# A recurrent-attention and Fourier-mix kernel: all engine streams in one list-scheduled order, with shared PSUM banks, a transposed state and sequential batches

## The chip, the cores and the metric

The kernel runs on one core of a Trainium2 chip. The metric is the device time of one execution in microseconds (us). A profile is one execution; its span is some 2 us shorter than the device time of the same run. Every timed comparison is made on one chip, beside runs of the kernel before.

The engines in the profile: PE is TensorE (matmuls), PEld its weight loads, DVE is VectorE, ACT is ScalarE, POOL is GpSimd, SP is the engine that issues most DMAs. Each works off its own stream of instructions in order.

## The reference, cut to what matters

For 4 batches, 8 heads, 768 time steps and head size 40, a recurrence with a 40x40 state per head:

```python
y[:, :, t] = einsum('bhd,bhde->bhe', rt, state)
Sa = einsum('bhde,bhe->bhd', state, at)
state = state * wt[:, :, None, :] - einsum('bhd,bhe->bhde', Sa, bt) + einsum('bhd,bhe->bhde', vt, kt)
```

Then, per batch, on x of 768x320 (the heads side by side): the real part of a two-dimensional Fourier transform is added to x, the rows are normalised, and an MLP (320 to 1280, relu, back to 320) is added.

## The kernel before

Both kernels split the 768 steps into 6 chunks of 128, so there are 24 chunks in all. For each chunk, **preparation** (no state needed) takes the logarithm of w, its running sum by a matmul with ones, the exponentials, scales k, b and a on GpSimd, transposes them on TensorE and forms three masked 128x128 products for each head. The **chain** (needs the state) solves for the chunk's corrections in two rounds, updates the state and gives y. When a batch is done, its **post** stage does Fourier transform, normalisation and MLP.

The parts that the argument touches:

```python
psP = ctx.enter_context(tc.tile_pool(name="psP", bufs=4, space=PSUM))
psA = ctx.enter_context(tc.tile_pool(name="psA", bufs=2, space=PSUM))
psM = ctx.enter_context(tc.tile_pool(name="psM", bufs=2, space=PSUM))
# ... preparation: decay row through DRAM, broadcast to 64 partitions, twice
nc.scalar.activation(flat(wl)[96:128], cum[96:128], Act.Exp)
nc.sync.dma_start(wd, wl[127:128].rearrange("p h d -> p (h d)"))
for e in range(2):
    nc.sync.dma_start(wm[i % 3][e * 64:(e + 1) * 64, :, e, :],
                      bass.AP(wd.tensor, wd.offset + e * D, [[0, 64], [2 * D, NP], [1, D]]))
# ... chain: new state, its bf16 copy, and the transposed copy that the next chunk's X needs
nc.vector.tensor_add(P, P, st[0])
nc.vector.tensor_tensor(s32, P, g["wm"], Alu.mult)
nc.scalar.copy(sc[:, :, :, :D], s32)
nc.tensor.transpose(...)                      # x4
nc.vector.tensor_copy(sT, pt)
# ... chain, last line: y of the chunk
nc.vector.tensor_tensor(xb[:, c, :], Y.rearrange("t h d -> t (h d)"), g["wp"], Alu.mult)
# ... the driver: batches 0 and 1 (then 2 and 3) interleaved, the second three chunks behind
order = []
for j in range(3 * (B + 1)):
    for sm in (0, 1):
        q = j - 3 * sm
        if 0 <= q < NCH * (B // 2):
            order.append((2 * (q // NCH) + sm, q % NCH))
for i, (bb, c) in enumerate(order):
    states[bb] = chain(bb, c, i, gs.pop(i), states[bb], xbs[bb], not pend)
    # ... load chunk i + 3, prepare chunk i + 2, two pieces of a pending post stage
```

The framework that builds the kernel reorders each engine's stream with a scheduler of its own; the written order guides it.

## Time and profile before

| | before |
|---|---|
| time, median (all runs) | 421.11 us (420.61 to 422.29) |
| span of the profile | 419.9 us |
| PE / DVE / ACT / POOL busy | 77% / 51% / 51% / 46% |
| mean granted TensorE clock | 0.877 |

First the engine table of the kernel before (busy us, share of the span, instructions), then two of the rows of the view in 40 slices (busy tenths of PE, and granted TensorE clock in tenths), one line of the DMA queues (packets, MB, share of 16 engines) and the shares of the chain of waits that ended last:

```profile
PE 325.0 (77%) x3636; PEld 223.0 (53%) x3636; DVE 215.2 (51%) x430; ACT 213.6 (51%) x448; POOL 191.8 (46%) x279
...
PE   1657778854887877788798787688798976998796
...
PEclk9996988895888896599899999659959998799999
...
q1 hardware_dynamic: 170728, 37.07, 45.5%
...
PE 35%; POOL 13%; DVE 12%; issue 10%; ACT 10%; DMA 3%; SPq 1%; POOLq 0%; ACTq 0%; DVEq 0%
```

No engine is full, and the chain that decides the time passes through all of them. The clock row shows stretches of 5 and 6, where TensorE was granted half its clock for most of a slice.

The last instruction of each chunk, the multiply by wp, marks progress. It starts first at 38.7 and last at 359.4 us. Cut there, the kernel has three stages.

The middle stage holds 23 chunk-to-chunk steps in 320.7 us, 13.9 us each, and TensorE is busy for 79% of it. The last stage is 60.5 us, when all recurrences are over.

What a step waits for is seen in the chain of waits in order of time (start us, length us, engine, what), here around 300 us of the kernel before:

```profile
300.32 1.08 ACT M_4890 L251 x2
...
301.54 0.26 POOL M_4890 L180
...
302.59 0.86 POOL t__91 L125
303.45 0.18 POOL t__91 L126
...
304.24 0.86 POOL t__91 L127
...
305.14 1.46 PE pt L143 x12
...
308.07 0.68 DVE A_4989 L161
```

It goes from the copies of M (chunk's chain) on ScalarE to its mask on GpSimd, then to GpSimd's three products for a *later* chunk, which stand behind that mask in GpSimd's stream, to that chunk's transposes, and to VectorE's masks. Preparation that needs no state waits behind chain work.

### The profile page before, as it was taken

How to read it: one execution, taken by the hardware profiler on the slowest of the kernel's cores; microseconds unless marked ns; L12 is line 12 of the kernel's file. 1: busy time of each engine (PE TensorE's matmuls, PEld its weight loads, DVE VectorE, ACT ScalarE, POOL GpSimd, SP SyncE). 2: the span in 40 equal slices, each digit the busy share in tenths (PEclk: the TensorE clock that was granted, in tenths of full speed). 3: DMA queues.
4: the chain of work that ended last, by engine and by line, in shares of the span. 5: the costliest groups of instructions: out<-in, count | busy, mean ns of one | idle time of the engine just before them, and what ended most of it. 6: DMA issues, size and time to landing. Idle time of an engine off the chain costs nothing.

```text
span 419.9 us, 9289 instructions
## 1 busy us (share of the span) xinstructions
PE 325.0 (77%) x3636; PEld 223.0 (53%) x3636; DVE 215.2 (51%) x430; ACT 213.6 (51%) x448; POOL 191.8 (46%) x279
## 2 busy tenths in 40 slices
PE   1657778854887877788798787688798976998796
PEld 0435455542666655645555565464574654556353
DVE  4342555796646477725515658854352568112611
ACT  2334546565545654574483675457455454742352
POOL 4886834671647652631523786443333355202100
PEclk9996988895888896599899999659959998799999
DMA  9999685852555755616506576323140300222011
GB/s 153 183 147 161 111 143 96 142 92 43 97 101 148 167 98 87 101 27 126 95 18 133 133 177 119 55 49 53 53 148 19 86 2 2 94 94 95 0 48 47
DMA packets 172435, 39.29 MB, mean 94 GB/s; under 512 B 161556, under 2 KB 172072, under 8 KB 172392
## 3 DMA queue, kind: packets, MB, share of 16 engines
q1 hardware_dynamic: 170728, 37.07, 45.5%
q0 software_dynamic: 1664, 1.64, 2.4%
q8 instruction: 28, 0.46, 0.4%
q14 instruction: 15, 0.12, 0.1%
HBM read 32.44 MB, written 7.89 MB: 96 GB/s over the span
## 4 chain that ended last, share of the span: by engine, by line
PE 35%; POOL 13%; DVE 12%; issue 10%; ACT 10%; DMA 3%; SPq 1%; POOLq 0%; ACTq 0%; DVEq 0%
PE ph L184 7%; PE po L184 7%; PE pt L143 4%; ACT hm L363 2%; PE X L184 2%; PE pt L355 1%; POOL t__103 L127 1%; POOL rs L343 1%; POOL t__103 L126 1%; ACT snT L248 1%; POOL t__97 L125 1%; DMA xd<-xb 1%; PE pt L238 1%; PE pt L246 1%; DMA x__4928<-in_w_dram 1%
## 5 line engine op out<-in xcount | busy, mean ns | idle before, releaser
L184 PE MATMUL ph<-unT,w1sb 128*128 128x384 bf16 x240 | 50.1, 340 | 3.7 <-ACT unT L356 1.3
L363 ACT ACTIVATE hm<-ph 128x384 bf16<-128x384 f32 x80 | 39.1, 494 | 19.5 <-PE ph L184 18.6
L155 ACT COPY vT<-pt 128x512 bf16<-128x512 bf16 x24 | 14.1, 587 | 53.4 <-PE pt L143 51.3
L184 PE MATMUL po<-w2sb,hm 128*128 128x320 bf16 x240 | 35.6, 299 | 0.2 <-ACT hm L363 0.2
L184 PEld LDWEIGHTS <-w1sb 128*128 128x128 bf16 x240 | 22.9, 102 | 22.3 <-issue 11.3
L122 DVE TENSOR_TENSOR wp<-cum,logw 128x320 f32<-128x320 f32 x24 | 11.7, 487 | 43.6 <-ACT rw L120 43.6
L374 DVE TENSOR_TENSOR ot<-po,u 128x320 f32<-128x320 f32 x24 | 11.8, 490 | 40.0 <-PE po L184 40.0
L143 PE MATMUL pt<-ident_78,t__91 128*128 128x128 bf16 x160 | 17.1, 263 | 17.0 <-POOL t__91 L125 7.9
L149 DVE COPY kbT<-pt 128x1024 bf16<-128x1024 bf16 x24 | 16.5, 689 | 22.3 <-PE pt L143 22.2
L184 PEld LDWEIGHTS <-hm 128*128 128x128 bf16 x240 | 22.5, 98 | 10.2 <-issue 0.7
L118 PE MATMUL cum<-logw,ut_ones 128*128 128x320 f32 x48 | 24.6, 601 | 4.3 <-ACT logw L116 4.3
L209 DVE TENSOR_TENSOR dx<-X,xs 128x320 bf16<-128x320 f32 x24 | 11.7, 488 | 28.0 <-PE X L184 24.5
L143 PEld LDWEIGHTS <-t__91 128*128 128x128 bf16 x160 | 11.9, 117 | 21.9 <-POOL t__91 L125 9.7
L143 PE MATMUL pt<-ident_78,t__103 128*128 128x128 bf16 x160 | 15.8, 250 | 9.9 <-POOL t__103 L127 3.6
L152 DVE COPY arT<-pt 128x1024 bf16<-128x1024 bf16 x24 | 16.6, 692 | 12.6 <-PE pt L143 12.6
L174 PEld LDWEIGHTS <-vT 64*128 64x128 bf16 x192 | 13.8, 100 | 15.2 <-issue 13.5
L143 PE MATMUL pt<-ident_78,t__97 128*128 128x128 bf16 x160 | 14.7, 244 | 6.5 <-POOL t__97 L127 2.5
L248 ACT COPY snT<-pt 128x512 bf16<-128x512 bf16 x24 | 14.1, 587 | 9.7 <-PE pt L246 9.1
L345 DVE TENSOR_SCALAR un<-u,mv,rs 128x320 bf16<-128x320 f32 x24 | 14.7, 654 | 8.0 <-POOL rs L343 8.0
L310 POOL COPY zzr<-zz 128x256 bf16<-128x256 bf16 x16 | 6.0, 399 | 27.9 <-ACT zz L307 27.9
L143 PEld LDWEIGHTS <-t__103 128*128 128x128 bf16 x160 | 11.2, 112 | 13.4 <-POOL t__103 L127 5.0
L174 PEld LDWEIGHTS <-kbT 64*128 64x128 bf16 x384 | 13.7, 108 | 8.2 <-DVE arT L152 4.1
(1032 smaller groups left out, 928.4 us busy)
## 6 DMA issues: line engine op xcount, KB each, us to landing
xd<-xb SPq DMA_DIRECT2D x4, 960.0 KB
u<-xd SPq DMA_DIRECT2D x24, 160.0 KB, 2.9
out_dram<-ot SPq DMA_DIRECT2D x24, 160.0 KB, 1.9
w2sb<-in_moe_w_ch_dram POOLq DMA_DIRECT2D x1, 800.0 KB, 10.7
w1sb<-in_moe_w_ch_dram POOLq DMA_DIRECT2D x2, 320.0 KB, 6.1
t__95<-wd SPq DMA_DIRECT2D x16, 40.0 KB, 4.1
t__101<-wd SPq DMA_DIRECT2D x12, 40.0 KB, 3.1
t__107<-wd SPq DMA_DIRECT2D x12, 40.0 KB, 4.2
```

What stands on the lines that cost most here:

```text
L118: nc.tensor.matmul(cum, ut_ones, logw)
L122: nc.vector.tensor_sub(wp, cum, logw)
L143: nc.tensor.transpose(pt[:, j, q, :], s_[:, 2 * q:2 * q + 2, :].rearrange("t h d -> t (h d)"), ident16)
L149: nc.vector.tensor_copy(kbT, pt)
L152: nc.vector.tensor_copy(arT, pt)
L155: nc.scalar.copy(vT, pt[:, 0])
L174: nc.tensor.matmul(ps[e][:, q, :], lT[e * 64:(e + 1) * 64, q, :], rT[e * 64:(e + 1) * 64, q, :], start=(q == 0), stop=True, skip_group_che ...
L184: nc.tensor.matmul(o, l_, r_, start=first, stop=True, skip_group_check=True)
L248: nc.scalar.copy(snT, pt)
L345: nc.vector.tensor_scalar(un[:, ti], u[:, ti], mv[:, ti, 0:1], rs[:, ti:ti + 1], Alu.subtract, Alu.mult)
L363: nc.scalar.activation(hm, ph, Act.Relu)
L374: nc.vector.tensor_tensor(ot, po, u[:, ti], Alu.add)
```

## The change

Intent: plan all five streams together. The kernel records each operation with its engine, an estimated occupancy, the buffers it reads and writes, and a rank. A list scheduler in the kernel then picks, again and again, the operation that can start first (within a window of 0.12 us the better rank wins), binds buffers, and emits. The framework's scheduler is switched off. With it come: eight PSUM banks in one pool (at most 4 for preparation, at most 3 for post), batches one after another, a state kept transposed, the decay summed on TensorE, and warm-up matmuls on zeros where the plan sees TensorE idle. The core of the diff, with cuts marked:

```diff
+            for e in self.ENG:
+                cand = []
+                for o in ready[e]:
+                    t = max(free[e], o.ready)
+                    # ... and not before its buffers come free
+                    if t < INF:
+                        cand.append((t, o.prio, o))
+                # ...
+                t0 = min(c[0] for c in cand)
+                t, _, o = min((c for c in cand if c[0] <= t0 + self.slack), key=lambda c: (c[1], c[0]))
+                if best is None or t < best[0]:
+                    best = (t, o)
 ...
+    ctx.enter_context(tc.manual_schedule())
-    psP / psA / psM  (4 + 2 + 2 banks)
+    ps = slots_ps = Slots([psum.tile([128, 512], FP32, tag=f"ps{i}", name=f"ps{i}") for i in range(8)],
+                          dict(prep=4, post=3))
+    P = Plan(0.12, warm)
 ...
-            nc.scalar.activation(flat(wl)[96:128], cum[96:128], Act.Exp)
-            nc.sync.dma_start(wd, ...)          # and two broadcast loads into wm
+            def sums():
+                for h in range(H):
+                    e, q = h % 2, h // 2
+                    nc.tensor.matmul(wl()[e * 64:e * 64 + D, q:q + 1], logw()[:, h * D:(h + 1) * D], one_c,
+                                     start=(q == 0), stop=True, skip_group_check=True)
+            op("PE", 0.4, sums, w=[wl], r=[logw])
+            # ... later: two exponentials of 40x4 on ScalarE, per partition of the transposed state
 ...
-                mm(P[:, q], v_pair, k_pair[:, :, :D], q == 0)       # state
+                mm(Q()[:, q], k_pair, v_pair[:, :, :D], ...)        # transposed state: X needs no copy
 ...
-    order: batches in skewed pairs
+    order = [(bb, c) for bb in range(B) for c in range(NCH)]
+            at(i - 1, 60)
+            lds[i + AH] = load(bb, c)
+            at(i, 40)
+            gs[i + AH] = prep(lds[i + AH], c, [sns[i - 1]] if i > 0 else [])
+        # ... at(2, 80): the tables; at(i, 0): chain; at(i + 1 ..., 70): post stage
```

## The prediction

> **What bounds the kernel now.** No engine is full: the engine table has TensorE matmul busy 77% of 419.9 us, VectorE 51%, ScalarE 51%, GpSimd 46%. The chain of waits passes through every engine: PE 35%, POOL 13%, DVE 12%, issue 10%, ACT 10%. In time order it is one ring per step: the copy of M on ScalarE, its mask on GpSimd, three GpSimd products for the chunk two ahead (0.85 us each), its transposes, VectorE copies and masks, the chain's matmuls. In-order queues tie preparation to recurrence. The group of the final multiply by wp starts first at 38.7 and last at 359.4 us: 13.9 us a step. The mean granted clock is 0.877, so about 103 us ran at half rate (4 us windows show 0.50 at 164-180 and 268-280). The Trainium skill, "TensorE: Matmul & The Clock Gate", Part 1, says that an idle window re-throttles TensorE to half rate; the trace agrees: PE was busy only 2.1 of 8 us just before the slow stretch at 96-104.
>
> **Tail.** After 359.4 us, 21 us go to the backlog of the third batch's MLP and 39 us to the last batch's post stage.
>
> **What changes.** Arithmetic is nearly the same.
> - Removed: 20 decay rows on ScalarE (0.43 us each), 20 stores and 40 broadcast loads of the decay (3.8 us to landing), which held the state update early on (4.5 and 3.4 us).
> - Added: 160 fp32 matmuls with 40-column weights and one moving column. The fp32 weight load of 128 columns takes 0.19 us, two a matmul, so I estimate 1 to 1.5 us a chunk, 20 to 30 us of TensorE; and 40 tiny activations, about as long as the rows removed. Warm-up matmuls: 68 before, 60 after.
> - Moved: all orders; batches run one after another, each post stage beside the next batch's first four steps; eight shared banks replace the 4+2+2.
>
> **New sum.** With trace durations: one chunk without post needs per engine about 6.5 us (VectorE 6.6, ScalarE 6.5, GpSimd 6.5, TensorE 6.5 to 7 at full clock and dense). The recurrence alone, from the state's bf16 copy to the next (four matmul bursts of about 0.35, three ScalarE copies of 0.44, three VectorE operations of 0.49, hops), is about 5 us, perhaps 8 with queueing, so sequential batches need not bind. A post stage adds about 26 us of TensorE, 16 ScalarE, 14 VectorE. TensorE bounds batches 2 to 4 at about 65 us each; at 87% density 75.
> - start to first chain: 16
> - batch 1 (tables on VectorE and GpSimd): 57
> - batches 2 to 4: 225
> - last post alone, now without backlog: 36
> - half-rate stretches and orders that don't fit real durations (weights sums, the 0.86 us power on GpSimd): 11
>
> Predicted: 345 us, 318 to 378. Chances: faster 0.96, same 0.03, slower 0.01.
>
> **What would show it right.** TensorE's busy share near 88 to 90%, clock at least 0.92, about 9 us a step in the first batch and 12 to 13 later (the wp multiply's start times), only 36 to 40 us after the last one, no decay transfers, DMA share lower. The chain of waits should be mostly PE.
>
> **What would make it wrong.** A fixed order planned with wrong durations makes every in-order queue wait at its head: then TensorE stays below 80% busy and the span is above 370. A recurrence over 12 us a step without post would show that sequential batches cost what interleaving hid. If loads lag at the start (DMA share above 1.0 to 30 us), batch 1 takes longer. If the sums cost only a few tenths of a microsecond, and density is above 92%, the time falls under 325.

## More of the kernel before

The view by windows for the kernel before (from:to, length; busy us and instructions of PE, PEld, DVE, ACT, POOL; clock; DMA share; GB/s):

```profile
core 0: us, PE busy (x) PEld busy (x) DVE busy (x) ACT busy (x) POOL busy (x), PEclk, DMA share, GB/s
0.00:38.70 38.70, 19.71 (x201) 13.07 (x201) 15.43 (x27) 14.06 (x29) 25.32 (x54) 0.91 1.07 166
38.70:359.40 320.70, 254.68 (x3113) 178.93 (x3113) 185.32 (x365) 174.22 (x366) 160.31 (x214) 0.85 0.47 90
359.40:419.90 60.50, 50.59 (x324) 30.99 (x322) 14.48 (x39) 25.37 (x56) 6.20 (x12) 0.98 0.19 66
```

## The result, and the profile after

The changed kernel took 327.07 us (median of 4 runs, 326.86 to 327.97), beside 420.86 us for the kernel before (418.54 to 422.29). The ratio is 0.778, with a 95% interval of 0.774 to 0.782. Ratios here are the mean time of one kernel's runs over that of the other's of the same rounds, so they are not quite the ratio of the medians quoted. Executions over 1.5% slower than the fastest of the same kernel are left out of the means. The time lies inside the predicted range of 318 to 378, 18 us below the predicted 345.

The same lines for the changed kernel (columns as above):

```profile
PE 284.0 (87%) x3948; PEld 203.9 (63%) x3948; DVE 218.4 (67%) x429; ACT 199.1 (61%) x468; POOL 193.5 (60%) x282
...
PE   6649875768899989999999999999997899978995
...
PEclk9985999676999999999999999999999999999999
...
q1 hardware_dynamic: 159808, 35.40, 54.3%
...
PE 47%; DVE 14%; ACT 6%; POOL 5%; issue 5%; DVEq 0%; ACTq 0%; POOLq 0%
```

The same stages for the changed kernel. Its first chunk ends at 35.0 us, the first batch (six chunks) at 91.9, the last chunk at 286.75:

```profile
0.00:35.00 35.00, 24.12 (x287) 15.89 (x288) 19.02 (x31) 13.29 (x32) 27.50 (x58) 0.85 1.02 167
35.00:91.90 56.90, 43.67 (x682) 30.79 (x684) 46.33 (x81) 35.81 (x81) 41.86 (x55) 0.85 0.80 137
91.90:286.75 194.85, 184.46 (x2761) 136.24 (x2758) 140.51 (x288) 134.93 (x323) 117.88 (x160) 1.00 0.50 108
286.75:324.80 38.05, 31.70 (x225) 21.02 (x223) 12.56 (x33) 15.07 (x34) 6.22 (x12) 1.00 0.24 79
```

| stage | before | after | difference |
|---|---|---|---|
| to the first chunk's end | 38.7 | 35.0 | -3.7 |
| 23 further chunks | 320.7 | 251.75 | -68.95 |
| after the last chunk | 60.5 | 38.05 | -22.45 |
| span | 419.9 | 324.8 | -95.1 |

In batches 2 to 4 (the third row) TensorE is busy for 184.46 of 194.85 us, 94.7%, at full clock, where the old middle stage left 21% idle. So this stage is taken to be bound by TensorE; e4 below tests it in part. TensorE's matmul busy time fell from 325 to 284 us although the real matmuls are the same and 160 small ones were added. One reason can be read off: the mean clock rose from 0.877 to 0.958. Windows of 4 us over the kernel before go down to a clock of 0.50 and no lower; with half rate as the low state that is an estimated 103 us of low clock before (419.9 x 0.123 x 2) and 27 us after. The Trainium skill, "Perfetto Trace Analysis", section "Identifying the Most-Contended Engine", warns that matmul busy time is a poor measure of headroom, because matmuls are pipelined, and prefers the share of peak FLOP/s and the busy share of weight loads. The two busy shares agree in direction here: weight loads rose from 53% to 63% of the span.

### The profile page after: what moved, and what is told of

Same layout as the page of the kernel before. It is cut to its first block, busy times and chain, and to the rows that moved or that the text cites. A ratio compares the mean times of both kernels' runs of the same rounds, so it can differ in the third digit from the quotient of the medians.

```text
span 324.8 us, 9858 instructions
## 1 busy us (share of the span) xinstructions
PE 284.0 (87%) x3948; PEld 203.9 (63%) x3948; DVE 218.4 (67%) x429; ACT 199.1 (61%) x468; POOL 193.5 (60%) x282
## 3 DMA queue, kind: packets, MB, share of 16 engines
q1 hardware_dynamic: 159808, 35.40, 54.3%
## 4 chain that ended last, share of the span: by engine, by line
PE 47%; DVE 14%; ACT 6%; POOL 5%; issue 5%; DVEq 0%; ACTq 0%; POOLq 0%
PE ps_219 L278 6%; PE ps_226 L278 5%; PE ps_223 L278 5%; PE ps_224 L278 4%; PE ps_220 L278 4%; PE ps_221 L278 3%; PE ps_222 L278 3%; PE ps_225 L278 3%; DVE un_191 L545 1%; PE ps_222 L294 1%; PE ps_225 L294 1%; DVE un_192 L545 1%; PE ps_221 L294 1%; PE ps_223 L294 1%; DVE pr_163 L367 1%
## 5 line engine op out<-in xcount | busy, mean ns | idle before, releaser
L278 PEld LDWEIGHTS <-w1sb 128*128 128x128 bf16 x240 | 21.5, 97 | 13.9 <-issue 1.2
L302 POOL TENSOR_SCALAR_AFFINE_SELECT pr_161<-pr_161 128x1024 bf16<-128x1024 bf16 x8 | 8.9, 1119 | 22.6 <-ACT pr_161 L431 12.0
L302 POOL TENSOR_SCALAR_AFFINE_SELECT pr_160<-pr_160 128x1024 bf16<-128x1024 bf16 x7 | 7.7, 1097 | 11.3 <-ACT pr_160 L431 10.1
L458 POOL TENSOR_TENSOR pm_173<-xb_172 128x320 bf16<-128x320 f32 x12 | 10.1, 861 | 3.2 <-DVE xb_172 L444 3.1
L458 POOL TENSOR_TENSOR pm_174<-xb_171 128x320 bf16<-128x320 f32 x12 | 10.1, 857 | 2.5 <-DVE xb_171 L444 2.4
L349 PEld LDWEIGHTS <-nat_91 128*128 128x128 bf16 x96 | 6.4, 105 | 8.2 <-POOL nat_91 L330 7.4
L302 POOL TENSOR_SCALAR_AFFINE_SELECT pr_159<-pr_159 128x1024 bf16<-128x1024 bf16 x6 | 7.3, 1214 | 6.8 <-ACT pr_159 L431 6.7
L302 POOL TENSOR_SCALAR_AFFINE_SELECT pr_164<-pr_164 128x1024 bf16<-128x1024 bf16 x7 | 7.7, 1095 | 4.6 <-ACT pr_164 L372 2.9
L349 PEld LDWEIGHTS <-nat_90 128*128 128x128 bf16 x96 | 6.1, 103 | 6.2 <-POOL nat_90 L330 5.6
L302 POOL TENSOR_SCALAR_AFFINE_SELECT pr_166<-pr_166 128x1024 bf16<-128x1024 bf16 x7 | 7.7, 1097 | 3.7 <-ACT pr_166 L372 2.4
L278 PEld LDWEIGHTS <-pm_174 128*128 128x128 bf16 x72 | 6.7, 110 | 2.6 <-POOL pm_174 L458 1.2
L260 PEld LDWEIGHTS <-ident_71 128*128 128x128 bf16 x60 | 5.4, 108 | 4.0 <-POOL ident_71 masks.py:199 2.0
L349 PEld LDWEIGHTS <-nat_92 128*128 128x128 bf16 x96 | 6.7, 109 | 1.7 <-POOL nat_92 L330 0.9
L278 PEld LDWEIGHTS <-pr_161 128*128 128x128 bf16 x136 | 5.5, 98 | 3.3 <-issue 1.4
L278 PEld LDWEIGHTS <-pr_159 128*128 128x128 bf16 x128 | 5.0, 97 | 3.7 <-POOL pr_159 L302 1.7
L294 PEld LDWEIGHTS <-kb_151 64*128 64x128 bf16 x128 | 4.3, 98 | 4.4 <-issue 3.3
L278 PEld LDWEIGHTS <-pm_173 128*128 128x128 bf16 x72 | 6.3, 108 | 0.8 <-issue 0.2
L349 PEld LDWEIGHTS <-nat_93 128*128 128x128 bf16 x96 | 6.2, 100 | 0.8 <-POOL nat_93 L330 0.5
L543 POOL TENSOR_TENSOR sm_213<-sm_213,mhalf 128x3 f32<-128x3 f32 x4 | 3.4, 853 | 5.6 <-DVE sm_213 L541 5.4
L302 POOL TENSOR_SCALAR_AFFINE_SELECT pr_163<-pr_163 128x1024 bf16<-128x1024 bf16 x5 | 5.5, 1094 | 2.0 <-ACT pr_163 L431 1.8
L278 PEld LDWEIGHTS <-pr_165 128*128 128x128 bf16 x128 | 5.3, 98 | 2.0 <-DVE pr_165 L367 0.7
L543 POOL TENSOR_TENSOR sm_215<-sm_215,mhalf 128x3 f32<-128x3 f32 x4 | 3.5, 873 | 5.1 <-DVE sm_215 L541 4.9
```

The source lines that it names most:

```text
L260: nc.tensor.matmul(ps.tiles[i][:, :m_], ident16, fill16[:, :m_], start=True, stop=True)
L278: nc.tensor.matmul(o, l_, r_, start=first, stop=True, skip_group_check=True)
L294: nc.tensor.matmul(ps2[e]()[:, q, :], lT[e * 64:(e + 1) * 64, q, :], rT[e * 64:(e + 1) * 64, q, :], start=(q == 0), stop=True, skip_group_ ...
L302: nc.gpsimd.affine_select(out=t_, in_=t_, compare_op=Alu.is_gt, fill=0.0, base=0, pattern=[[0, 2], [0, NP], [1, 128]], channel_multiplier=-1)
L349: nc.tensor.transpose(pt()[:, x_, q, :], nt()[:, j, 2 * q:2 * q + 2, :].rearrange("t h d -> t (h d)"), ident16)
L458: op("POOL", 0.82, lambda i_=i_, f_=f_: nc.gpsimd.tensor_tensor(pm()[:, i_, c - 3], xb()[:, c - 3], xb()[:, c], f_), w=[pm[(i_, c)]], r=[x ...
```

## The experiments

Unless said otherwise each run is the changed kernel with one edit, planned anew where the edit touches the plan. All twelve gave correct results. Their times stand beside the kernel before of their own rounds.

| run | edit | median us | ratio to before, 95% |
|---|---|---|---|
| (changed kernel) | | 327.07 | 0.778, 0.774 to 0.782 |
| e1_sched | framework's scheduler on | 373.65 | 0.889, 0.884 to 0.895 |
| e9_sched_pin | the same, sines pinned | 346.07 | 0.824, 0.818 to 0.829 |
| e10_sched_prog | the same, written order, no warm-up | 397.78 | 0.947, 0.941 to 0.953 |
| e5_before_seq | kernel before, sequential batches | 432.58 | 1.029, 1.021 to 1.038 |
| e2_inter | batches interleaved | 325.93 | 0.775, 0.771 to 0.780 |
| e3_oldstate | old state, decay by DMA | 329.21 | 0.784, 0.779 to 0.789 |
| e4_sums3 | decay sums three times | 332.06 | 0.792, 0.786 to 0.799 |
| e6_nofill | no warm-up matmuls | 331.94 | 0.786, 0.779 to 0.793 |
| e7_banks | banks 4 + 2 + 2 | 321.59 | 0.763, 0.758 to 0.768 |
| e8_tab | tables ranked later | 322.49 | 0.766, 0.761 to 0.771 |
| e11_best | e7, e8 and durations | 321.99 | 0.765, 0.760 to 0.771 |
| e12_slack | plan window 0.16 us | 323.93 | 0.770, 0.764 to 0.776 |

### Is it the order? (e1, e9, e10)

The theory: the order in which work stands in the streams is the main gain. The rival: the shorter recurrence, the decay sums and the banks are, and any order will do.

```diff
-    ctx.enter_context(tc.manual_schedule())
```

> Only the planned order is given up: the same operations and buffers, but the framework's own scheduler may reorder each engine's stream, as it did in the kernel before. Theory A (the planned order across the in-order queues is the main gain): above 370 us, TensorE busy share at 80% or less. Rival B (the shorter recurrence, decay sums and shared banks are the main gain, and any order will do): below 345 us.

It came to 373.65 us, but the run had a fault of its own. The groups of instructions of e1_sched show activation table loads that the changed kernel has not (line, engine, operation, count, busy us, mean ns, idle before):

```profile
L311 ACT ACT_TABLE_LOAD x16 | 20.5, 1283 | 0.3
...
L324 ACT ACT_TABLE_LOAD x15 | 19.2, 1283 | 4.1 <-PE ps L313 3.8
```

The framework had pulled the sines apart, so 36 more table loads, about 46 us of ScalarE, were built in. The run tells nothing about order, and was repeated with the sines and the reload pinned together:

```diff
-    ctx.enter_context(tc.manual_schedule())
-            nc.scalar.activation(tw12..., Act.Sin, ...)
+            pin = tc.keep_in_program_order
+            pin(nc.scalar.activation(tw12..., Act.Sin, ...))        # and the others, and the reload
```

> Repeats e1 without its fault: there the framework's scheduler pulled the sine activations apart and the build put 36 more activation table loads of 1.28 us each on ScalarE (about 46 us). Here the sines and the reload are pinned together, as the kernel before pins them; only the order of each engine's stream is the framework's. Theory A (the planned order itself is worth more than the rest): above 345 us. Rival B (structure and the emission order suffice; e1 was slow through the table loads): below 335 us.

It came to 346.07 us, 19 us over the changed kernel, and so only just on theory A's side. The pin held the sines in order, but its trace has five table loads against the changed kernel's three, one for an exponential that came between two sines and one to go back. The windows of e9_sched_pin, cut at its first and last chunk ends:

```profile
0.00:48.00 48.00, 26.39 (x287) 19.56 (x288) 19.64 (x33) 14.66 (x34) 34.72 (x72) 0.70 1.01 165
48.00:305.90 257.90, 231.59 (x3446) 167.86 (x3446) 180.20 (x366) 175.00 (x403) 151.71 (x198) 0.98 0.51 104
305.90:343.40 37.50, 31.01 (x218) 20.35 (x216) 11.65 (x33) 14.87 (x34) 6.14 (x12) 1.00 0.24 79
```

Of the 19 us, 13 lie before the first chunk's end (48.0 against 35.0 us) and 6 in the chunks after it (257.9 against 251.75). The clock before the first chunk's end was 0.70 against 0.85. The framework's scheduler, given the operations in the plan's order, keeps nearly all of it in the steady part.

Next, the same structure, but handed over in the written order, by rank alone:

```diff
-                t, _, o = min((c for c in cand if c[0] <= t0 + self.slack), key=lambda c: (c[1], c[0]))
-                if best is None or t < best[0]:
+                t, _, o = min(cand, key=lambda c: c[1])
+                if best is None or o.prio < best[1].prio:
                     best = (t, o)
-    P = Plan(0.12, warm)
+    P = Plan(0.12, None)
-    ctx.enter_context(tc.manual_schedule())          # and the pins of e9
```

> Framework scheduler with sines pinned, as e9, and the operations handed to it strictly in the written order (chain, preparation two ahead, post stage), which is how the kernel before is written; no warm-up matmuls. Structure, sequential batches, decay sums, transposed state and shared banks stay as in the changed kernel. Theory A (the plan is nearly the whole gain): 385 us or more. Rival B (the structure carries a large part): below 370 us.

It came to 397.78 us. The windows of e10_sched_prog, after its first chunk's end:

```profile
36.20:356.60 320.40, 254.11 (x3447) 188.36 (x3447) 186.40 (x370) 182.70 (x405) 160.53 (x216) 0.88 0.45 89
356.60:395.60 39.00, 29.48 (x204) 19.23 (x201) 11.60 (x33) 14.90 (x34) 6.08 (x12) 0.94 0.24 80
```

The 23 further chunks take 320.4 us, as in the kernel before (320.7), with TensorE busy 79% again; only the last stage is shorter, 39.0 against 60.5 us. This equality doesn't mean that the new state, decay and banks do nothing in a written order. e10 runs its batches one after another and the kernel before does not, and that alone costs the kernel before 33 us in this stage (e5, next). Against e5 the new structure is 34 us shorter there (354.1 to 320.4) and 35 us in all (432.58 to 397.78, and the same by the ratios), so two effects cancel. Which part of the structure brings it, and what small differences between the two written orders add, was not tested.

What the planned order brings with the new structure and sequential batches in place is seen between e10 and the changed kernel: 320.4 to 251.75, 69 us of this stage. Of these, TensorE's idle time makes up 43 us (66.3 to 23.6) and its busy time 26 (254.11 to 228.13), at a clock of 0.88 against 0.97; how much of the clock is itself a result of the denser order was not tested apart. e10 lacks the warm-up matmuls too, but the profiled run of e6, the changed kernel without them, takes 252.1 us in this stage. In the medians the step from e10 to e9 (order of emission, with the warm-up) is 52 us, and keeping the order exactly is 19 more.

### Sequential batches, in both kernels (e5, e2)

```diff
     # in the kernel before
-    order = [...skewed pairs...]
+    order = [(bb, c) for bb in range(B) for c in range(NCH)]
```

> The kernel before with one line changed: batches one after another instead of in skewed pairs. Theory A (sequential batches alone do not gain; order must change with it): within 5% of the kernel before or slower, because the ring through the in-order queues stays. Rival D (sequential batches are the gain): below 385 us.

It came to 432.58 us, 3% slower than the kernel before. Its windows after the first chunk's end:

```profile
38.70:392.80 354.10, 283.83 (x3189) 194.54 (x3194) 184.74 (x368) 185.31 (x388) 160.04 (x214) 0.80 0.43 83
392.80:434.40 41.60, 32.77 (x222) 20.79 (x220) 12.53 (x35) 15.02 (x34) 6.21 (x12) 0.99 0.25 84
```

The last stage falls to 41.6 us: the third batch's MLP is no longer left over. But the 23 further chunks take 354.1 us instead of 320.7. TensorE's granted clock in this stage is 0.80 against 0.85; why one batch alone waits longer in this order was not traced. The rival that sequential batches are the gain falls.

The reverse, in the changed kernel:

```diff
-    order = [(bb, c) for bb in range(B) for c in range(NCH)]
+    order = [...skewed pairs, as before...]
```

> The changed kernel with the batches interleaved in pairs again (skewed by three chunks, as before), order planned anew by the same list scheduler. Theory A: sequential batches are not what gains; they help only because the post stages spread and no backlog of post work is left at the end, so this run is 10 to 25 us slower than the changed kernel, with a tail after the last multiply by wp of 50 us or more. Rival C (the recurrence of one batch binds the sequential kernel, interleaving would hide it): this run is 5 us or more faster.

It came to 325.93 us, a ratio of 0.775 against 0.778: no difference. Neither expectation was met. The windows of e2_inter after the first chunk's end:

```profile
35.00:277.10 242.10, 214.89 (x3353) 159.86 (x3356) 184.54 (x364) 165.43 (x392) 158.18 (x213) 0.95 0.58 116
277.10:323.90 46.80, 40.65 (x288) 27.42 (x289) 14.50 (x38) 20.02 (x45) 6.22 (x12) 1.00 0.25 82
```

Interleaved, the further chunks take 242.1 us, 9.7 less than in the changed kernel, and the last stage 46.8 us, 8.75 more. With a plan, the choice of batch order shifts work between middle and end and gains nothing.

### The state and the decay (e3, e4)

e3 puts back the old state, the transpose and copy in the recurrence, and the decay row through DRAM:

```diff
-            op("PE", 0.4, sums, w=[wl], r=[logw])
+            op("ACT", ACT(320), lambda: nc.scalar.activation(flat(wl())[96:128], cum()[96:128], Act.Exp), ...)
+            op("SP", 0.3, ...)     # wd <- wl, then two broadcast loads into wt
-            mm(Q()[:, q], k_pair, v_pair)          # and X from the direct copy, Y from the transposed one
+            mm(Q()[:, q], v_pair, k_pair)          # and X from the transposed copy, Y from the direct one
-    in_s = slots("in", 20, ...)
+    in_s = slots("in", 18, ...)                    # room for the wider decay tiles
```

> The changed kernel with the old state: not transposed, decay row from ScalarE through DRAM and two broadcast loads, and the PE transpose and VectorE copy back in the recurrence. Adds about 1.1 us to the recurrence of each of 20 chunks (0.4 transposes, 0.42 copy, two hops) and a DMA trip of about 8 us that preparation two chunks ahead should hide. Theory A: 5 to 15 us slower than the changed kernel, since only the first batch is near the recurrence limit. Rival B (the short recurrence is the main gain): 25 us or more slower.

It came to 329.21 us, about 2 us over the changed kernel, and the intervals overlap. That is below what was expected. The window of e3_oldstate from its first to its last chunk's end:

```profile
31.30:289.60 258.30, 227.12 (x3232) 163.34 (x3235) 188.27 (x373) 176.73 (x390) 161.39 (x217) 0.97 0.64 122
```

The 23 further chunks take 6.5 us more than in the changed kernel, and the first chunk ends 3.7 us sooner. So under a plan the longer recurrence and the DMA trip are hidden for the most part, and not wholly.

e4 does the eight sums three times:

```diff
+                for _ in range(3):
                     for h in range(H):
                         nc.tensor.matmul(wl()...)  # the same eight sums, same result
```

> The eight decay sums of each chunk are done three times (same result), 320 more small fp32 matmuls; the plan does not know. The trace of the changed kernel shows 16 loads and matmuls of one chunk starting within 0.35 to 0.5 us, so two more passes are about 0.9 us a chunk, 18 us of TensorE over 20 chunks. If TensorE bounds: 8 to 18 us slower. If the sums' estimate in the prediction (1 to 1.5 us a chunk) were right, 40 us or more slower. If TensorE is not the limit: under 4 us.

It came to 332.06 us; by the ratios (0.792 less 0.778, of 419.39 us) 6 us over the changed kernel, between the two expectations (under 4 us if TensorE is not the limit, 8 to 18 if it is). In the profiles the 23 further chunks take all of it, 257.76 against 251.75 us. TensorE's busy time rose from 284.0 to 295.2 us for 40 more passes, 0.28 us a pass, and about half of these 11 us shows in the time. So a pass costs a few tenths of a microsecond, not 1 to 1.5. The chain of waits of the changed kernel shows one directly:

```profile
213.94 0.63 PE ps_226 L314 x2
214.57 0.40 PE ps_221 L322 x16
214.97 0.30 PE ps_222 L278 x8
```

Sixteen instructions take 0.40 us, 25 ns each, between two matmul groups.

### Warm-up, banks, tables (e6, e7, e8, e11), and the plan's scatter (e12)

e6 leaves the warm-up matmuls away:

```diff
-    P = Plan(0.12, warm)
+    P = Plan(0.12, None)
```

> The changed kernel without its 57 warm-up matmuls on zeros. They sit nearly all in the first batch and the tail. If they hold the clock: granted clock falls from 0.958 to about 0.90 and the time rises by 5 to 12 us. If dense real work holds it: within 3 us of the changed kernel, same clock outside the first 85 us.

Its four runs are 327.47, 331.78, 332.09 and 333.56 us, with clocks of 0.951, 0.907, 0.928 and 0.923. The 333.56 is counted as slow and stays out of the ratio of 0.786. The intervals overlap. The profile is of the 327.47 run, whose last chunk ends at 286.79 us, as in the changed kernel (286.75). So the warm-up is worth between nothing and about 5 us in the fast runs; more is not shown.

e7 divides the banks as before:

```diff
-                          dict(prep=4, post=3))
+                          dict(prep=4, acc=2, post=2))
     # transposes and M's products move from group "acc", the post stage's transposes from "post", to "prep"
```

> The changed kernel with the eight PSUM banks divided as before: 4 for preparation, transposes and products, 2 for X, Q and Y, 2 for the post stage. Order planned anew for that. Theory A: 3 to 15 us slower, mostly in the tail and the overlapped post stages, where ScalarE's relu must free one of two banks. If banks are what held the kernel before: 30 us or more slower.

It came to 321.59 us, faster rather than slower. Shared banks are not a gain of this change.

e8 came from the changed kernel's first batch, where the fourth and fifth chunks took 15.0 and 13.4 us. VectorE's stream there (timeline: start us, length us, engine, line, operation, shapes), four of the passes that wrap the angles of the Fourier tables:

```profile
46.73 1.37 DVE L609 TENSOR_SCALAR u_178<-xb_171 128x768 f32<-128x768 f32 x1
...
51.67 1.06 DVE L611 TENSOR_SCALAR u_178<-u_178 128x768 f32<-128x768 f32 x1
52.77 1.08 DVE L613 TENSOR_TENSOR xb_171<-xb_171,u_178 128x768 f32<-128x768 f32 x1
...
56.39 1.50 DVE L613 TENSOR_TENSOR xb_171<-xb_171,u_178 128x768 f32<-128x768 f32 x1
```

And GpSimd's in the same time:

```profile
51.23 1.10 POOL L302 TENSOR_SCALAR_AFFINE_SELECT pr_164<-pr_164 128x1024 bf16<-128x1024 bf16 x1 [0.57 <-ACT pr_164 L431]
...
53.00 1.81 POOL L302 TENSOR_SCALAR_AFFINE_SELECT pr_159<-pr_159 128x1024 bf16<-128x1024 bf16 x1
...
57.02 1.18 POOL L333 CAST nat_91<-in_131 128x320 bf16<-128x320 f32 x1
```

The mask of a 128x1024 tile takes 1.10 us at 51.23 and 1.81 us at 53.00; the copy of 128x320 takes 1.18 us at 57.02, and 0.44 us elsewhere in this run. The Trainium skill, "SBUF — State Buffer", section "Who interferes with whom", states that VectorE and GpSimd share one pair of SBUF ports under an exclusive lock. The lines agree with it: the two slow operations start while a table addition with both inputs in SBUF is under way (52.77 and 56.39), and end 1.0 and 0.3 us after it; no run tested the lock by itself. The plan ranked this table work above chunks 3 to 5 (counting from zero), so it went first there.

```diff
-            at(2, 80)
+            at(5, 75)
             tables()
```

> The changed kernel with the table work ranked behind the recurrence of the first five chunks instead of ahead of chunks 3 to 5. In the changed kernel the tables' VectorE passes take most of VectorE from 46.7 to 68.4 us, while GpSimd's operations there rise from 0.86 to as much as 1.42 us, and the first batch ends at 82.7 us. Theory: the first batch ends 3 to 10 us sooner and the whole is 2 to 8 us faster. If the tables only move, no difference within 1%.

(The 82.7 us that the expectation takes for the first batch's end is that of its fifth chunk; the sixth starts its last multiply at 91.9 us.) Three runs are 321.26, 322.36 and 322.62 us. The fourth, the profiled one, took 616.09 us and is told below. For where the time went, the profile of e11 serves, which has the same edit, the bank division and corrected durations:

```diff
     # e7 and e8, and in the plan:
-            op("POOL", 0.25, ...pow...)
+            op("POOL", 0.85, ...pow...)
-            op("DVE", DVE(hi - lo, 2), ...)        # two table passes; the third likewise from DVE(n)
+            op("DVE", DVE(hi - lo), ...)           # to 2 * DVE(n)
```

> The changed kernel with the three finds together: banks divided as in e7, tables ranked behind the first five chunks as in e8, and the plan's durations corrected where the trace differs (0.85 us for the power on GpSimd[...]). If the gains of e7 (5.5 us) and e8 (4.5 us) add: 314 to 318 us. If both only shake the plan by chance: 320 to 328 us.

It came to 321.99 us: the finds do not add. In e11 the fifth chunk ends at 72.7 us, 9.4 earlier than in the changed kernel (82.2), but the sixth at 90.9 against 91.9. The chain of waits of e11_best between 80 and 88 us shows why (start us, length us, what; L653 and L659 with no tile are table loads):

```profile
80.40 1.28 ACT L653
...
81.69 1.03 ACT tw L653
...
85.32 1.28 ACT L659
...
86.62 0.48 ACT wp L327
...
87.17 0.87 POOL nat L330
...
88.08 0.61 PE ps L349 x4
```

The sines and their two table loads hold ScalarE for 6.2 us; wp's exponential (L327) stands behind them, and preparation waits for it. Ranking the tables later moved the wait, and did not remove it.

Are the 1.5% of e7, e8 and e11 more than another draw of the plan? e12 changes one constant of the planner:

```diff
-    P = Plan(0.12, warm)
+    P = Plan(0.16, warm)
```

> The changed kernel with one constant of its planner changed (the window in which a higher rank wins over an earlier start, 0.12 to 0.16 us): the same work, another plan of the same kind. It asks how far two such plans differ by chance. If the plan's scatter is small: 326 to 329 us, and the 1.5% of e7, e8 and e11 are effects of their edits. If the scatter is of their size: outside 324 to 331 us, and those three finds are not shown to be more than another draw of the plan.

It came to 323.93 us, a ratio of 0.770. That is outside the 326 to 329 us set for a small scatter, and by 0.07 us outside the 324 to 331 beyond which the scatter was to count as large; its interval overlaps those of the changed kernel, e7, e8 and e11. Differences of 1% among re-planned kernels can be chance, so the causes given for e7 and e8 are not shown. As versions, e7, e8 and e11 are faster than both kernels that were compared.

The odd run of e8 needs a word. The run is listed with a granted clock of 1.0, but its page has no clock row and its trace no clock record. Its matmuls run slowly, while VectorE's 128x320 addition takes its usual 0.49 us. From its timeline, 25 down-projection matmuls and 30 up-projection ones:

```profile
574.37 9.61 PE L278 MATMUL ps<-w2sb,h 128*128 128x320 bf16 x25
...
585.11 13.66 PE L278 MATMUL ps<-unT,w1sb 128*128 128x384 bf16 x30
```

That is 384 and 455 ns each. The chain of waits of the changed kernel has ten down-projections in 1.36 us and three up-projections in 0.49 us: 136 and 163 ns. Already at 220 us nine up-projections took 4.17 us. The Trainium skill, "TensorE: Matmul & The Clock Gate", section "Seeing it yourself", warns that clock events in traces have been unreliable and the gate stuck at a low rate. That the clock went unrecorded agrees with the first; that the gate was stuck is not shown. It happened once in all runs, and no conclusion rests on it.

## Why the prediction was right

The predicted time was 345 us, in a range of 318 to 378; measured were 327. The sum's terms against the spans of the profile:

| term | predicted | measured |
|---|---|---|
| start and first batch | 16 + 57 = 73 | 91.9 |
| batches 2 to 4 | 225 (75 each) | 194.85 (65 each) |
| last post stage alone | 36 | 38.05 |
| reserve for low clock and misplanned work | 11 | not seen apart |

- "TensorE bounds batches 2 to 4 at about 65 us each; at 87% density 75" was the wrong step, too cautious by 30 us. TensorE's work was 61.5 us a batch (184.46 over 3) and not 65, and the density 94.7% and not 87%: the plan left almost no holes, and the clock was 1.00 for the whole stage. That the span came to 65 us a batch, the figure for full density, is a coincidence of the two.
- "1 to 1.5 us a chunk, 20 to 30 us of TensorE" for the decay sums was mis-sized: one pass takes 0.40 us in the chain of waits, and 0.28 us of busy time in e4. The prediction added up lengths of weight loads (from 0.19 us for 128 columns). The loads and matmuls overlap here: a load is shown as some 0.12 us long and a matmul as 0.18 us, and 16 of each pass in 0.40 us. What counts is the start-to-start time of 25 ns. The Trainium skill, "TensorE: Matmul & The Clock Gate", section "Wait — 56ns, not 53.3ns?", gives about 25 ns as the floor from start to start however small a matmul is, and the trace agrees. The prediction would have come closer by using it.
- "Batch 1 (tables on VectorE and GpSimd): 57" and "start to first chain: 16" were too short together by 19 us. The windows show DMA at 102% of its share up to 35.0 us, and the prediction had named late loads there as a risk. After that a step took 11.4 us (56.9 over 5) instead of the expected 9, with the two long steps among the table work. In the batches after it a step took 10.8 us (194.85 over 18) instead of the expected 12 to 13.
- "Last post alone, now without backlog: 36" was right (38.05), and e5 shows that sequential batches do this: 41.6 us in the kernel before with that one line changed.
- "Sequential batches need not bind" was right: with the plan, interleaving changes nothing (e2). That they do cost without a plan (e5, 33 us in the middle stage) the prediction did not say.
- "In-order queues tie preparation to recurrence" was the reason given for the old 13.9 us a step. e10 and e9 support it: with the new structure in place, the plan's order takes the middle stage from 320.4 to 251.75 us. The structure is not nothing without a plan, which the prediction did not see: 35 us from e5 to e10. Which single wait binds a step in the old order was read from the chain and not tested.
- Clock at least 0.92: 0.958. PE busy "near 88 to 90%": 87%. A chain mostly PE: 47%, from 35%. "DMA share lower" was wrong as a share (45.5% to 54.3% for the main queue), though the bytes fell from 37.07 to 35.40 MB: the span shrank more.
- Of its conditions for a time under 325, both held (sums at a few tenths of a microsecond, density above 92%); the time was 327 because the first batch was 19 us longer.
- Two readings in the prediction were wrong. The clause that is cut gave 2.1 us of TensorE work in the 8 us before the slow stretch near 96 us; those 8 us are 92 to 100, half inside it. The clock was 1.00, 1.00, 0.95 and 0.50 in the four windows of 1 us from 92 to 96, with 0.51, 0.27, 0.19 and 0.00 us of matmuls: it fell after a sparse stretch, and no run isolates an idle one. And the 4.5 us for which the state update was "held" end at 98.7 us, where VectorE had worked through table passes and masks without a pause, not at a decay load; a decay load held it only at 31.2 us, for 2.1 us.

So the mechanism was right, and errors of opposite sign in the sizes, +19 and -41 (and +2 in the tail), left 20 us too much in the sum. That they cancelled by half is luck.

## What to carry to other kernels

Where no engine is full and the chain of waits wanders over all of them, look at what stands behind what in each in-order stream: here, with the new structure in place, the planned order took 69 us off the middle stage, while a shorter recurrence, other banks and another batch order, undone one at a time, changed the median by 2, -5.5 and -1 us once the order was planned. Ask each question in both settings: the same structure was worth 35 us in the written order. The plan on the old structure as a whole was not run. Cost a burst of small instructions by their start-to-start time in a trace, and not by the length of one. And before believing a 1% gain in a kernel whose order comes from a planner, change a constant that should not matter and see how far the time moves.

## What the Trainium skill lacked or had wrong

- "TensorE: Matmul & The Clock Gate" has the 25 ns floor for matmuls, but no figure for pairs of a small fp32 weight load and a matmul; here a pass of 16 such matmuls with 40-column fp32 weights took 0.40 us in the chain, although each load is shown as some 0.12 us long and each matmul as 0.18 us.
- "TensorE: Matmul & The Clock Gate" tells of a gate stuck at a quarter of the clock for 50 us or more; here matmuls were at 2.8 times their length (384 against 136 ns), and so from 220 us at the latest to the end of the run at 614 us, with no clock record. Whether this is the same event is not shown.
